# Attention and feed-forward on one core: full fp32 products as three float32r products, and the layer tiles shared out anew between VectorE and GpSimd

## The chip, the cores and the metric

The kernel runs on one core of a Trainium2 chip. TensorE (PE in the profile) multiplies matrices into PSUM; VectorE (DVE), ScalarE (ACT) and GpSimd (POOL) do elementwise work; SyncE (SP) issues the transfers. The metric is the device time of one execution in microseconds; of the kernel before it is the median of three runs.

## The reference

```python
# q: (4, 12288, 128), kv: (4, 384, 32, 128), w_sr: (128, 128)
kv_pool = kv.reshape(B, H // r, r, W // r, r, C).mean(axis=(2, 4))   # r = 4: 768 keys
k = v = kv_pool.reshape(B, -1, C) @ w_sr
s = scale * (q @ k.transpose(0, 2, 1))
a = softmax(s)
x = (a @ v).reshape(-1, 128)
# w_in: (128, 2048), w_out: (2048, 128)
h = x @ w_in
out = (h - tanh(h)) @ w_out
```

There are 4 batches of 12288 queries; keys and values are the same 768 vectors.

## The kernel before, in words

The 49152 queries go through in 96 groups of 512 (24 a batch, `G = 512`, `NG = 24`), always with channels on the 128 partitions. The kernel treats both the softmax and the layer as a main linear part and a small rest. The scores are small, so exp(s) - 1 - s is what remains beside a linear part; and h - tanh(h) is expanded around the batch's centre, with a linear part (slopes), and a third-order rest.

Small rests are multiplied in float32r, which reads 32-bit data at a lower precision; the two linear parts need more, and are multiplied in full fp32. So a group has on TensorE:

- scores (L712): 6 matmuls of 512 columns from the keys `kTr` and the rounded query `qr`, into three two-bank PSUM tiles `big`. ACT forms exp (L716, `E`), VectorE the rest E - 1 - s (L719, `r2`).
- shares (L732): 6 matmuls that sum the rest over the keys; ACT turns the sum into `t` (L745).
- the attention's straight part (L736, `straight` in `attention`): **one full fp32 matmul** from the moment matrix `Mn` and the unrounded query `qs` (tile `q`), and 6 float32r matmuls of the values (L741) into the same PSUM bank. VectorE multiplies with `t` (L751): the output's difference from the centre, `dl`. GpSimd rounds it to float32r, `dr` (L754).
- forth (L792): 16 matmuls from the scaled weights `winr` and `dr`, two to a `big` tile, hence 8 layer tiles of 128x1024. For each, r = h^2 (1 + h) is formed in one of two ways. On VectorE: ACT squares (L796, `u`), VectorE does the rest in one instruction (L799, `r`). On GpSimd: ACT copies out of PSUM (L803, `v`), GpSimd adds 1 (L806) and multiplies twice (L810, `z` and `rp`).
- back (L832): 16 matmuls of `Wr` with those tiles, and the layer's straight part (L780): **one full fp32 matmul** from the slopes `A` and `dl`, all into the bank `acc`. ACT adds the centre's value (L841) and SP stores the group's output.

`ON_POOL` says which layer tiles go to GpSimd: tiles 0 and 3 of groups with an even number, tile 0 of groups with an odd number, and tile 0 alone of group 94: 143 tiles in all.

The order on each engine is written by a planner (`Plan`) before the program is built. Every operation has a step (its due time, in units of a layer tile; a group is 8 steps), an engine, and an estimated duration. The planner runs these through a list schedule: an engine takes, of what can start within 0.15 us, the operation with the earliest step. GpSimd's operations and some of VectorE's are kept apart by a shared "port". The order that comes out is fixed; on the chip each engine works through it and waits on semaphores. `BUFS` gives the number of buffers of each tag; tiles of one tag form a ring in which a new tile waits until the one as many places before has been used up. Tiles of different meaning can share a tag. PSUM has three `big` tiles, one bank `x` and one bank `acc`.

Attention of group g begins 20 steps before the layer of group g. The preparation of a batch (`keys`: pooling on VectorE and GpSimd, the centred keys, the values `vv32` and `vvr`, the moment `Mn` at L446 and L450; `about_centre`: weights scaled for this centre, `winr`, `Wr`, `Wg`, and the slopes `A` in four parts, L661 to L669) is spread over the groups of the batch before it. For the first batch it forms the kernel's start. After a check of the inputs a second, general program (`any_inputs`) would run where the expansion does not hold; it doesn't run on these inputs.

Of the kernel before, what the change touches and what calls it, by code (L numbers as in the profile page):

```python
# [9 lines left out]
F32 = mybir.dt.float32  # L10
R32 = mybir.dt.float32r
# [4 lines left out]
ALU = mybir.AluOpType  # L16
# [130 lines left out]
def attention_then_ffn(ctx: ExitStack, tc: tile.TileContext, q, kv, w_sr, w_in, w_out, out):  # L147
    nc = tc.nc
    V, A, PL, PE, SP = nc.vector, nc.scalar, nc.gpsimd, nc.tensor, nc.sync
# [7 lines left out]
    NGT = B * NG  # L157
# [5 lines left out]
    dram = ctx.enter_context(tc.tile_pool(name="dram", bufs=1, space=DRAM))  # L163
    plan = Plan(tc)

    BUFS = {"kc": 2, "kvp": 1, "kTr": 2, "vv32": 1, "vvr": 2, "Mn": 2, "A": 2, "Wg": 4, "Wr": 2,
            "winr": 2, "q": 4, "qr": 3, "E": 2, "r2": 5, "t": 2, "dl": 2, "dr": 2, "u": 3, "r": 4,
            "rp": 2, "v": 2, "z": 1, "o": 2, "row": 2, "col": 2, "G0": 2, "hb": 2, "W2": 1,
            "most": 1}

    def sb(key, tag, shape, dt=F32, step=0.0):
        n = BUFS[tag]
        plan.tile(key, tag, n, lambda: wk.tile(shape, dt, tag=tag, name=tag, bufs=n), step)
# [166 lines left out]
    def keys(b, s0):  # L340
# [107 lines left out]

        def copy_moment():
            A.activation(out=plan[Mn], in_=plan[pm][:, 0:P], func=AF.Copy, scale=scale / K)  # L450
# [14 lines left out]
        plan.op(s2, "ACT", 0.85, copy_values, (pv,), (vv32,), late=0.1)  # L465
        plan.op(s2 + (0 if b else 2), "DVE" if b else "ACT", 0.9, small_values, (pv,), (vvr,))
        plan.op(s3, "PE", 1.8, moment, (vv32,), (pm,), late=0.2)
        plan.op(s3, "ACT", 0.3, copy_moment, (pm,), (Mn,), late=0.1)
        norm(s4, Mn, p4, b)

    def about_centre(b, s0):
# [178 lines left out]
        for n in range(NW):  # L650
# [20 lines left out]
            def by_third(n=n, fs=fs):  # L671
# [7 lines left out]
            plan.op(third_at[n], "POOL", 1.25, by_third,  # L679
                    (a3s, ("wout32", n)), ((Wr, n),), port=True)  # L680

    def attention(g, s0):
        b, i = divmod(g, NG)
        kTr, vvr, Mn = (f"{x}.{b}" for x in ("kTr", "vvr", "Mn"))
        qs, qr, dl, dr, den, num, t = (f"{x}.{g}" for x in ("q", "qr", "dl", "dr", "den", "num", "t"))
        sb(qs, "q", [P, G])
        sb(qr, "qr", [P, G], R32)
        sb(t, "t", [P, G])
        sb(dl, "dl", [P, G])
        sb(dr, "dr", [P, G], R32)  # L690
        plan.tile(f"left.{g}", f"left.{g}", 1, lambda: None)

        def load_q():
            SP.dma_start(out=plan[qs], in_=q[b, :, i * G : (i + 1) * G])

        def rounded_q():
            PL.tensor_scalar(out=plan[qr], in0=plan[qs], scalar1=1.0, scalar2=1.0, op0=ALU.mult,
                             op1=ALU.mult)

        plan.op(s0 - 10, "SP", 0.5, load_q, (), (qs,), late=2.0, dma=0.65)  # L700
        plan.op(s0 - 3, "POOL", 0.63, rounded_q, (qs,), (qr,))
        for k in range(AN):
            s, e, r = (f"{x}.{g}.{k}" for x in ("s", "e", "r2"))
            at = s0 + k * ATT / AN
            big(s, at)
            sb(e, "E", [P, WIDE])
            sb(r, "r2", [P, WIDE], R32)

            def scores(k=k, s=s):
                for h in range(2):  # L710
                    n = 2 * k + h
                    PE.matmul(out=half(plan[s], h), lhsT=plan[kTr][:, n * P : (n + 1) * P],  # L712
                              rhs=plan[qr], start=True, stop=True)

            def exps(s=s, e=e):
                A.activation(out=plan[e], in_=plan[s], func=AF.Exp)  # L716

            def beyond(s=s, e=e, r=r):
                V.scalar_tensor_tensor(out=plan[r], in0=plan[e], scalar=-1.0, in1=plan[s],  # L719
                                       op0=ALU.add, op1=ALU.subtract)  # L720
# [13 lines left out]

        def straight():
            PE.matmul(out=plan[num], lhsT=plan[Mn], rhs=plan[qs], start=True, stop=False)  # L736

        def values(k):
            for h in range(2):
                n = 2 * k + h  # L740
                PE.matmul(out=plan[num], lhsT=plan[vvr][:, n], rhs=half(plan[f"r2.{g}.{k}"], h),  # L741
                          start=False, stop=(n == KT - 1))

        def share_left():
            A.activation(out=plan[t], in_=plan[den], func=AF.Copy, scale=-1.0, bias=1.0)  # L745

        def store_left():
            SP.dma_start(out=left[g : g + 1], in_=plan[t][0:1, :])

        def apart():  # L750
            V.tensor_tensor(out=plan[dl], in0=plan[num], in1=plan[t], op=ALU.mult)  # L751

        def rounded():
            PL.tensor_scalar(out=plan[dr], in0=plan[dl], scalar1=1.0, scalar2=1.0, op0=ALU.mult,  # L754
                             op1=ALU.mult)

        for k in range(AN):
            plan.op(at, "PE", 0.465, partial(shares, k), ("ident", f"r2.{g}.{k}"), (den,), late=0.2)
        plan.op(at, "ACT", 0.69, share_left, (den,), (t,), late=0.1)
        plan.op(at + 1, "SP", 0.5, store_left, (t,), (f"left.{g}",), late=2.0, dma=0.02)  # L760
        plan.op(at + 0.5, "PE", 0.93, straight, (Mn, qs), (num,))
        for k in range(AN):
            plan.op(at + 0.5, "PE", 0.465, partial(values, k), (vvr, f"r2.{g}.{k}"), (num,), late=0.2)
        plan.op(at + 0.5, "DVE", 0.69, apart, (num, t), (dl,), late=0.08)
        plan.op(at + 1, "POOL", 0.63, rounded, (dl,), (dr,))

    FS, AS, WS, APART, MORE = 3, 8, 6, 3, 3.0
    ON_POOL = [((0, 3), (0,))[g % 2] for g in range(NGT)]
    ON_POOL[NGT - 2] = (0,)

    def feed_forward(g, s0):
        b = g // NG
        Am, Wr, G0, winr, dl, dr = (f"{x}.{k}" for x, k in (
            ("A", b), ("Wr", b), ("G0", b), ("winr", b), ("dl", g), ("dr", g)))
        acc, o = f"acc.{g}", f"o.{g}"
        bank(acc, "acc", s0)
        sb(o, "o", [P, G])

        def straight():
            PE.matmul(out=plan[acc], lhsT=plan[Am], rhs=plan[dl], start=(g > 0), stop=(g == 0))  # L780

        if g:
            plan.op(s0, "PE", 0.93, straight, (Am, dl), (acc,))
        for n in range(UN):
            hp, u, r, v, z = (f"{x}.{g}.{n}" for x in ("h", "u", "r", "v", "z"))
            s = s0 + n - (2 if n in ON_POOL[g] else 0)
            big(hp, s)

            def forth(n=n, hp=hp):
# [21 lines left out]

            plan.op(s - 6, "PE", 0.465, forth, (winr, dr), (hp,), late=0.2)
            back_at = s + 2
            if n in ON_POOL[g]:
                sb(r, "rp", [P, WIDE], R32)
                sb(v, "v", [P, WIDE])
                sb(z, "z", [P, WIDE])
                plan.op(s, "ACT", 1.03, copy, (hp,), (v,), late=0.1)
                plan.op(s, "POOL", 1.05, moved_pool, (v,), (z,))
                plan.op(s, "POOL", 2.4, partial(times, z, z, v), (z, v), (z,))  # L820
                plan.op(s, "POOL", 2.4, partial(times, r, z, v), (z, v), (r,))
                back_at = s + 5
# [122 lines left out]
    def any_inputs():  # L945
        def t(tag, shape, dt=F32):
            return wk.tile(shape, dt, tag=tag, name=tag + "_any", bufs=BUFS[tag])

        def bank():
            return ps.tile([P, WIDE], F32, tag="big", name="big_any", bufs=3)  # L950
# [4 lines left out]
        for b in range(B):  # L955
# [161 lines left out]
```

## Time and profile before

| what | value |
|---|---|
| median of three runs | 1421.43 us (1420.7 to 1421.87) |
| profiled execution, its own time | 1421.67 us |
| its span, first to last instruction | 1419.9 us |
| TensorE, matmul records | 1388.5 us busy, 98% |
| VectorE | 1216.1 us, 86% |
| ScalarE | 1158.2 us, 82% |
| GpSimd | 1066.2 us, 75% |
| mean granted TensorE clock | 0.996 of full speed |

Busy is the union of an engine's instruction records. Records of neighbours can overlap: a matmul's record begins before the one ahead of it has ended, so the spacing of starts says more than the length of a record. A full fp32 matmul shows as two records, a float32r one as one. "Idle before" is the time in which an engine had nothing running ahead of an instruction, with the instruction that ended the wait behind the arrow. In a timeline the columns are start, duration, engine, line, operation, output and inputs by tile name, number of merged instructions.

### The profile page before, as it was taken

The page shows a single profiled execution, that of the slowest core. Times are in us where ns is not written, and L with a number is a line of the kernel's source. Part 1 is how long each engine was busy: PE and PEld are TensorE (multiplying, and loading weights), DVE is VectorE, ACT ScalarE, POOL GpSimd, SP SyncE. Part 2 cuts the span into 40 slices and gives each one's busy share as a digit, 9 for nine tenths or more (in the row PEclk, how much of TensorE's full clock was granted, in tenths as well). Part 3 has the DMA queues.
Part 4 walks back from the last instruction along what each step waited for, and adds up shares of the span by engine and source line. Part 5 has one row for each costly group of instructions (what it writes and reads, how often), then busy time and mean ns, then how long its engine had stood idle before and what let it go on. Part 6 is the DMA issues. An engine that isn't in the chain of part 4 may idle for free.

```text
span 1419.9 us, 17460 instructions
## 1 busy us (share of the span) xinstructions
PE 1388.5 (98%) x5824; PEld 1039.0 (73%) x5824; DVE 1216.1 (86%) x1203; ACT 1158.2 (82%) x1299; POOL 1066.2 (75%) x826
## 2 busy tenths in 40 slices
PE   5999999999999999999999999999999999999997
PEld 4777777777777777777777777777777777777775
DVE  7978888888988887898988888888888888888886
ACT  4768887887888888787888888877888888888886
POOL 3788676788887676788986776698667777876773
PEclk9999999999999999999999999999999999999999
DMA  9231111012321111124211111111110111111101
GB/s 357 75 119 38 45 38 38 30 60 82 127 89 38 38 39 36 36 81 138 81 52 45 38 38 38 34 57 46 38 44 32 45 40 37 45 38 38 38 17 37
DMA packets 40370, 84.53 MB, mean 60 GB/s; under 512 B 5232, under 2 KB 7408, under 8 KB 40272
## 3 DMA queue, kind: packets, MB, share of 16 engines
q1 hardware_dynamic: 40272, 83.34, 17.6%
q8 instruction: 48, 0.79, 0.2%
q14 instruction: 50, 0.41, 0.1%
HBM read 57.93 MB, written 25.39 MB: 59 GB/s over the span
## 4 chain that ended last, share of the span: by engine, by line
PE 87%; POOL 5%; DVE 4%; ACT 2%; issue 1%; DMA 0%; SPq 0%; DVEq 0%; POOLq 0%; ACTq 0%
PE big L792 24%; PE acc L832 23%; PE x L741 9%; PE x L732 9%; PE big L712 8%; PE acc L780 6%; PE x L736 5%; POOL z L810 2%; DVE r L799 1%; POOL rp L810 1%; PE x L559 1%; PE x L661 1%; POOL z L806 1%; DVE kvp L369 1%; DVE r L719 0%
## 5 line engine op out<-in xcount | busy, mean ns | idle before, releaser
L799 DVE SCALAR_TENSOR_TENSOR r<-big,u 128x1024 fp32r<-128x1024 f32 x625 | 752.9, 1219 | 117.4 <-ACT u L796 87.1
L796 ACT ACTIVATE u<-big 128x1024 f32<-128x1024 f32 x625 | 636.7, 1031 | 144.0 <-PE big L792 140.4
L792 PE MATMUL big<-dr,winr 128*128 128x512 f32 x1536 | 522.8, 423 | 3.4 <-DVE r L799 2.2
L832 PE MATMUL acc<-r,Wr 128*128 128x512 f32 x1250 | 399.7, 404 | 0.8 <-DVE r L799 0.8
L719 DVE SCALAR_TENSOR_TENSOR r<-E,big 128x1024 fp32r<-128x1024 f32 x288 | 349.4, 1214 | 45.6 <-ACT E L716 42.7
L792 PEld LDWEIGHTS big<-dr,winr 128*128 128x128 f32 x1536 | 277.2, 188 | 127.9 <-DVE r L799 31.3
L806 POOL TENSOR_SCALAR z<-v 128x1024 f32<-128x1024 f32 x143 | 152.4, 1065 | 272.9 <-ACT v L803 270.3
L810 POOL TENSOR_TENSOR rp<-z,v 128x1024 fp32r<-128x1024 f32 x143 | 344.4, 2408 | 9.4
L810 POOL TENSOR_TENSOR z<-z,v 128x1024 f32<-128x1024 f32 x143 | 345.4, 2416 | 7.5
L716 ACT ACTIVATE E<-big 128x1024 f32<-128x1024 f32 x288 | 296.9, 1032 | 41.6 <-PE big L712 38.8
L832 PEld LDWEIGHTS acc<-r,Wr 128*128 128x128 f32 x1250 | 233.8, 188 | 67.0 <-issue 13.9
L712 PE MATMUL big<-qr,kTr 128*128 128x512 f32 x576 | 187.8, 408 | 0.0
L741 PE MATMUL x<-r,vvr 128*128 128x512 f32 x576 | 184.9, 403 | 0.0
L732 PE MATMUL x<-r,share 128*128 128x512 f32 x576 | 181.5, 398 | 0.4 <-DVE dl L751 0.4
L803 ACT COPY v<-big 128x1024 f32<-128x1024 f32 x143 | 145.3, 1016 | 30.2 <-PE big L792 28.0
L741 PEld LDWEIGHTS x<-r,vvr 128*128 128x128 f32 x576 | 108.2, 188 | 30.2 <-issue 6.7
L712 PEld LDWEIGHTS big<-qr,kTr 128*128 128x128 f32 x576 | 103.9, 188 | 35.8 <-DVE r L799 8.6
L732 PEld LDWEIGHTS x<-r,share 128*128 128x128 f32 x576 | 108.2, 188 | 28.0 <-issue 2.4
L832 PE MATMUL acc<-rp,Wr 128*128 128x512 f32 x286 | 102.2, 439 | 1.1 <-POOL rp L810 0.7
L780 PE MATMUL acc<-dl,A 128*128 128x512 f32 x192 | 101.0, 607 | 0.0
L736 PE MATMUL x<-q,Mn 128*128 128x512 f32 x192 | 98.1, 592 | 0.7 <-ACT t L745 0.7
L832 PEld LDWEIGHTS acc<-rp,Wr 128*128 128x128 f32 x286 | 53.0, 188 | 25.5 <-issue 13.9
(159 smaller groups left out, 818.6 us busy)
## 6 DMA issues: line engine op xcount, KB each, us to landing
q<-in_q_dram SPq DMA_DIRECT2D x96, 256.0 KB
out_dram<-o SPq DMA_DIRECT2D x96, 256.0 KB
kc<-in_kv_dram SPq DMA_DIRECT2D x38, 512.0 KB
r<-in_kv_dram SPq DMA_DIRECT2D x8, 512.0 KB
kc<-inverse SPq DMA_DIRECT2D x12, 256.0 KB
u<-in_moe_w_in_dram SPq DMA_DIRECT2D x3, 512.0 KB
u<-in_moe_w_out_dram SPq DMA_DIRECT2D x3, 512.0 KB
left<-t SPq DMA_DIRECT2D x96, 2.0 KB
```

Source lines behind the costliest of these rows:

```text
L712: PE.matmul(out=half(plan[s], h), lhsT=plan[kTr][:, n * P : (n + 1) * P], rhs=plan[qr], start=True, stop=True)
L716: A.activation(out=plan[e], in_=plan[s], func=AF.Exp)
L719: V.scalar_tensor_tensor(out=plan[r], in0=plan[e], scalar=-1.0, in1=plan[s], op0=ALU.add, op1=ALU.subtract)
L732: PE.matmul(out=plan[den], lhsT=share, rhs=half(plan[f"r2.{g}.{k}"], h), start=(n == 0), stop=(n == KT - 1))
L736: PE.matmul(out=plan[num], lhsT=plan[Mn], rhs=plan[qs], start=True, stop=False)
L741: PE.matmul(out=plan[num], lhsT=plan[vvr][:, n], rhs=half(plan[f"r2.{g}.{k}"], h), start=False, stop=(n == KT - 1))
L780: PE.matmul(out=plan[acc], lhsT=plan[Am], rhs=plan[dl], start=(g > 0), stop=(g == 0))
L792: PE.matmul(out=half(plan[hp], h), lhsT=plan[winr][:, f * P : (f + 1) * P], rhs=plan[dr], start=True, stop=True)
L796: A.activation(out=plan[u], in_=plan[hp], func=AF.Square)
L799: V.scalar_tensor_tensor(out=plan[r], in0=plan[hp], scalar=1.0, in1=plan[u], op0=ALU.add, op1=ALU.mult)
L810: PL.tensor_tensor(out=plan[to], in0=plan[x], in1=plan[y], op=ALU.mult)
L832: PE.matmul(out=plan[acc], lhsT=plan[Wr][:, f], rhs=half(plan[r], h), start=(g == 0 and f == 0), stop=(g > 0 and f == FT - 1))
```

## The change

A value x is split into an upper part, x rounded to float32r, and a lower part, x minus the upper part, also in float32r. A product of two such values is then formed as upper x upper + lower x upper + upper x lower, three float32r matmuls into the same bank; lower x lower is left out.

- Attention: `Mn` is split into `Mh` (ACT copies the upper part, GpSimd subtracts); the query's upper part is the `qr` that exists already, its lower part `ql` is subtracted on GpSimd, due four steps after `qr`.
- Layer: the slopes `A` are split into `Ah`, once a batch; the difference, now `df` from VectorE, has the upper part `dr` (as before) and the lower part `dl`, subtracted on GpSimd.
- Each group has two more GpSimd instructions of 128x512; the planner's durations are 1.1 us for each, and 0.7 us instead of 0.93 for a straight product.
- `ON_POOL` is tile 0 in every group: 96 layer tiles on GpSimd, the others on VectorE.
- Buffers: `qr` 4 for 3, `Wg` 3 for 4, `Mn` 1 for 2, `dl` 1 for 2; new `Mh` 2, `Ah` 2, `ql` 2, `df` 1; `vv32` loses its own buffer and takes one of the ring `kc`, in which the keys' chunks arrive. The general program takes its `vv32` from the ring `r`.

```diff
-    BUFS = {"kc": 2, "kvp": 1, "kTr": 2, "vv32": 1, "vvr": 2, "Mn": 2, "A": 2, "Wg": 4, "Wr": 2,
-            "winr": 2, "q": 4, "qr": 3, "E": 2, "r2": 5, "t": 2, "dl": 2, "dr": 2, "u": 3, "r": 4,
+    BUFS = {"kc": 2, "kvp": 1, "kTr": 2, "vvr": 2, "Mn": 1, "Mh": 2, "A": 2, "Ah": 2, "Wg": 3, "Wr": 2,
+            "winr": 2, "q": 4, "qr": 4, "ql": 2, "E": 2, "r2": 5, "t": 2, "dl": 1, "df": 1, "dr": 2, "u": 3, "r": 4,
...
-        sb(vv32, "vv32", [P, KT, C])
+        sb(vv32, "kc", [P, KT, C])
...
         def copy_moment():
             A.activation(out=plan[Mn], in_=plan[pm][:, 0:P], func=AF.Copy, scale=scale / K)
+            A.copy(out=plan[Mh][:, 0], in_=plan[Mn])
+
+        def moment_left():
+            PL.tensor_tensor(out=plan[Mh][:, 1], in0=plan[Mn], in1=plan[Mh][:, 0].bitcast(F32),
+                             op=ALU.subtract)
...
-        plan.op(s3, "ACT", 0.3, copy_moment, (pm,), (Mn,), late=0.1)
+        plan.op(s3, "ACT", 0.65, copy_moment, (pm,), (Mn, Mh), late=0.1)
+        plan.op(s3, "POOL", 0.35, moment_left, (Mn, Mh), (Mh,))
...
+        def upper_slopes():
+            A.copy(out=plan[Ah][:, 0], in_=plan[Am])
+
+        def lower_slopes():
+            PL.tensor_tensor(out=plan[Ah][:, 1], in0=plan[Am], in1=plan[Ah][:, 0].bitcast(F32),
+                             op=ALU.subtract)
+
+        joined = slopes_at[3] + (APART if b else 1) + 0.1
+        plan.op(joined, "ACT", 0.3, upper_slopes, (Am,), (Ah,), late=0.1)
+        plan.op(joined, "POOL", 0.35, lower_slopes, (Am, Ah), (Ah,))
...
         def straight():
-            PE.matmul(out=plan[num], lhsT=plan[Mn], rhs=plan[qs], start=True, stop=False)
+            upper, lower = (plan[Mh][:, n] for n in range(2))
+            for n, (x, y) in enumerate(((upper, qr), (lower, qr), (upper, ql))):
+                PE.matmul(out=plan[num], lhsT=x, rhs=plan[y], start=(n == 0), stop=False)
+
+        def lower_q():
+            PL.tensor_tensor(out=plan[ql], in0=plan[qs], in1=plan[qr].bitcast(F32),
+                             op=ALU.subtract)
...
         def apart():
-            V.tensor_tensor(out=plan[dl], in0=plan[num], in1=plan[t], op=ALU.mult)
+            V.tensor_tensor(out=plan[df], in0=plan[num], in1=plan[t], op=ALU.mult)
...
-        plan.op(at + 0.5, "PE", 0.93, straight, (Mn, qs), (num,))
+        plan.op(s0 + 1, "POOL", 1.1, lower_q, (qs, qr), (ql,))
+        plan.op(at + 0.5, "PE", 0.7, straight, (Mh, qr, ql), (num,))
...
-        plan.op(at + 0.5, "DVE", 0.69, apart, (num, t), (dl,), late=0.08)
-        plan.op(at + 1, "POOL", 0.63, rounded, (dl,), (dr,))
+        plan.op(at + 0.5, "DVE", 0.69, apart, (num, t), (df,), late=0.08)
+        plan.op(at + 1, "POOL", 0.63, rounded, (df,), (dr,))
+
+        def lower_left():
+            PL.tensor_tensor(out=plan[dl], in0=plan[df], in1=plan[dr].bitcast(F32), op=ALU.subtract)
+
+        plan.op(at + 6, "POOL", 1.1, lower_left, (df, dr), (dl,))
...
-    ON_POOL = [((0, 3), (0,))[g % 2] for g in range(NGT)]
-    ON_POOL[NGT - 2] = (0,)
+    ON_POOL = (0,)
...
         def straight():
-            PE.matmul(out=plan[acc], lhsT=plan[Am], rhs=plan[dl], start=(g > 0), stop=(g == 0))
+            upper, lower = (plan[Ah][:, n] for n in range(2))
+            for n, (x, y) in enumerate(((upper, dr), (lower, dr), (upper, dl))):
+                PE.matmul(out=plan[acc], lhsT=x, rhs=plan[y], start=(g > 0 and n == 0),
+                          stop=(g == 0 and n == 2))
...
-            plan.op(s0, "PE", 0.93, straight, (Am, dl), (acc,))
+            plan.op(s0, "PE", 0.7, straight, (Ah, dl, dr), (acc,))
```

More of the change, by code (lines that the diff above doesn't have):

```diff
@@ L374, in keys @@
         sb(kTr, "kTr", [P, K], R32)
-        sb(vv32, "vv32", [P, KT, C])
+        sb(vv32, "kc", [P, KT, C])
         sb(vvr, "vvr", [P, KT, C], R32)
         sb(Mn, "Mn", [P, C])
+        Mh = f"Mh.{b}"
+        sb(Mh, "Mh", [P, 2, C], R32)
         apart_by = 4 if b else 1
@@ L481, in about_centre @@
         sb(Am, "A", [P, C])
+        Ah = f"Ah.{b}"
+        sb(Ah, "Ah", [P, 2, C], R32)
         sb(Wr, "Wr", [P, FT, C], R32)
@@ L680, in about_centre @@
                     (a3s, ("wout32", n)), ((Wr, n),), port=True)
+        def upper_slopes():
[6 more added lines that the diff above has]
+        plan.op(joined, "POOL", 0.35, lower_slopes, (Am, Ah), (Ah,))
     def attention(g, s0):
         b, i = divmod(g, NG)
-        kTr, vvr, Mn = (f"{x}.{b}" for x in ("kTr", "vvr", "Mn"))
+        kTr, vvr, Mh = (f"{x}.{b}" for x in ("kTr", "vvr", "Mh"))
         qs, qr, dl, dr, den, num, t = (f"{x}.{g}" for x in ("q", "qr", "dl", "dr", "den", "num", "t"))
@@ L687, in attention @@
         sb(qr, "qr", [P, G], R32)
+        ql = f"ql.{g}"
+        sb(ql, "ql", [P, G], R32)
         sb(t, "t", [P, G])
-        sb(dl, "dl", [P, G])
+        sb(dl, "dl", [P, G], R32)
+        df = f"df.{g}"
+        sb(df, "df", [P, G])
         sb(dr, "dr", [P, G], R32)
@@ L750, in apart @@
         def apart():
-            V.tensor_tensor(out=plan[dl], in0=plan[num], in1=plan[t], op=ALU.mult)
+            V.tensor_tensor(out=plan[df], in0=plan[num], in1=plan[t], op=ALU.mult)
         def rounded():
-            PL.tensor_scalar(out=plan[dr], in0=plan[dl], scalar1=1.0, scalar2=1.0, op0=ALU.mult,
+            PL.tensor_scalar(out=plan[dr], in0=plan[df], scalar1=1.0, scalar2=1.0, op0=ALU.mult,
                              op1=ALU.mult)
@@ L760, in attention @@
         plan.op(at + 1, "SP", 0.5, store_left, (t,), (f"left.{g}",), late=2.0, dma=0.02)
-        plan.op(at + 0.5, "PE", 0.93, straight, (Mn, qs), (num,))
+        plan.op(s0 + 1, "POOL", 1.1, lower_q, (qs, qr), (ql,))
+        plan.op(at + 0.5, "PE", 0.7, straight, (Mh, qr, ql), (num,))
         for k in range(AN):
             plan.op(at + 0.5, "PE", 0.465, partial(values, k), (vvr, f"r2.{g}.{k}"), (num,), late=0.2)
-        plan.op(at + 0.5, "DVE", 0.69, apart, (num, t), (dl,), late=0.08)
-        plan.op(at + 1, "POOL", 0.63, rounded, (dl,), (dr,))
+        plan.op(at + 0.5, "DVE", 0.69, apart, (num, t), (df,), late=0.08)
[3 more added lines that the diff above has]
+        plan.op(at + 6, "POOL", 1.1, lower_left, (df, dr), (dl,))
     FS, AS, WS, APART, MORE = 3, 8, 6, 3, 3.0
-    ON_POOL = [((0, 3), (0,))[g % 2] for g in range(NGT)]
-    ON_POOL[NGT - 2] = (0,)
+    ON_POOL = (0,)
     def feed_forward(g, s0):
         b = g // NG
-        Am, Wr, G0, winr, dl, dr = (f"{x}.{k}" for x, k in (
-            ("A", b), ("Wr", b), ("G0", b), ("winr", b), ("dl", g), ("dr", g)))
+        Ah, Wr, G0, winr, dl, dr = (f"{x}.{k}" for x, k in (
+            ("Ah", b), ("Wr", b), ("G0", b), ("winr", b), ("dl", g), ("dr", g)))
         acc, o = f"acc.{g}", f"o.{g}"
@@ L779, in straight @@
         def straight():
-            PE.matmul(out=plan[acc], lhsT=plan[Am], rhs=plan[dl], start=(g > 0), stop=(g == 0))
+            upper, lower = (plan[Ah][:, n] for n in range(2))
+            for n, (x, y) in enumerate(((upper, dr), (lower, dr), (upper, dl))):
+                PE.matmul(out=plan[acc], lhsT=x, rhs=plan[y], start=(g > 0 and n == 0),
+                          stop=(g == 0 and n == 2))
         if g:
-            plan.op(s0, "PE", 0.93, straight, (Am, dl), (acc,))
+            plan.op(s0, "PE", 0.7, straight, (Ah, dl, dr), (acc,))
         for n in range(UN):
             hp, u, r, v, z = (f"{x}.{g}.{n}" for x in ("h", "u", "r", "v", "z"))
-            s = s0 + n - (2 if n in ON_POOL[g] else 0)
+            s = s0 + n - (2 if n in ON_POOL else 0)
             big(hp, s)
@@ L813, in feed_forward @@
             back_at = s + 2
-            if n in ON_POOL[g]:
+            if n in ON_POOL:
                 sb(r, "rp", [P, WIDE], R32)
@@ L837, in feed_forward @@
         if g == 0:
-            plan.op(s0 + UN + 1, "PE", 0.93, straight, (Am, dl), (acc,), late=0.2)
+            plan.op(s0 + UN + 1, "PE", 0.7, straight, (Ah, dl, dr), (acc,), late=0.2)
         def result():
@@ L966, in any_inputs @@
             A.activation(out=halves(kT), in_=halves(pk)[:, :, 0:KH], func=AF.Copy, scale=scale / W)
-            pv, vv = bank(), t("vv32", [P, KT, C])
+            pv, vv = bank(), t("r", [P, KT, C])
             for n in range(KT):
```

## The prediction

> **What bounds the kernel now.** I read the page first (busy shares, chain), then busy time by stretch, then the orders of TensorE, VectorE and GpSimd in a steady stretch, then waits.
>
> ```profile
> span 1419.9 us, 17460 instructions
> ...
> PE 1388.5 (98%) x5824; PEld 1039.0 (73%) x5824; DVE 1216.1 (86%) x1203; ACT 1158.2 (82%) x1299; POOL 1066.2 (75%) x826
> ...
> PE 87%; POOL 5%; DVE 4%; ACT 2%; issue 1%; DMA 0%; SPq 0%; DVEq 0%; POOLq 0%; ACTq 0%
> ```
>
> The profiled execution took 1421.67 us, 1.8 more than its span and 0.24 above the median of the three runs; my sum starts at 1421.67. PE is busy 98% and is 87% of the chain, but matmul records overlap, so the share alone proves nothing; the spacing of their starts does. By stretch (columns: window, length, then busy time and count of PE, PEld, DVE, ACT, POOL):
>
> ```profile
> 1060.10:1383.50 323.40, 323.40 (x1309) 241.23 (x1309) 283.12 (x255) 280.34 (x313) 238.57 (x161) 1.00 0.11 37
> 224.10:362.50 138.40, 136.93 (x612) 103.80 (x612) 116.38 (x119) 109.48 (x123) 107.10 (x94) 1.00 0.19 59
> ...
> 527.60:679.40 151.80, 150.83 (x670) 115.18 (x669) 130.61 (x132) 119.58 (x134) 122.12 (x107) 1.00 0.23 73
> ...
> 870.00:1020.00 150.00, 149.14 (x666) 114.48 (x665) 124.84 (x127) 118.89 (x133) 114.85 (x96) 1.00 0.13 41
> ```
>
> The first row is a steady stretch without preparation, the others are the three in which the next batch's keys and weights are prepared. Starts on PE in the steady one:
>
> ```profile
> 1100.85 1.02 PE L780 MATMUL acc<-dl,A 128*128 128x512 f32 x2
> 1101.31 1.02 PE L832 MATMUL acc<-rp,Wr 128*128 128x512 f32 x2
> 1102.17 1.02 PE L736 MATMUL x<-q,Mn 128*128 128x512 f32 x2
> 1102.63 1.02 PE L792 MATMUL big<-dr,winr 128*128 128x512 f32 x2
> 1103.49 0.63 PE L832 MATMUL acc<-r,Wr 128*128 128x512 f32 x2
> ...
> 1106.27 0.62 PE L832 MATMUL acc<-r,Wr 128*128 128x512 f32 x2
> ...
> 1113.68 1.11 PE L780 MATMUL acc<-dl,A 128*128 128x512 f32 x2
> ...
> 1127.64 0.59 PE L780 MATMUL acc<-dl,A 128*128 128x512 f32 x1
> ```
>
> From 1103.49 to 1106.27 six pairs of float32r matmuls start in 2.78 us: 0.463 a pair, 0.232 each. From 1100.85 to 1102.17 stands one full product (L780, two records) and one pair, 1.32 us; from 1102.17 to 1103.49 the other (L736) and a pair, 1.32 again. So a full fp32 product takes 1.32 - 0.463 = 0.857 us. A group has 50 float32r matmuls (6 scores, 6 shares, 6 values, 16 forth, 16 back) and two full ones: 50 x 0.232 + 2 x 0.857 = 13.31 us. The two groups from 1100.85 to 1127.64 take 26.79, 13.40 each. PE has work for 99% of the steady time at the spacing it reaches: it is the bound.
>
> **The change, part by part.**
>
> Straight products (L736, L780). Three float32r matmuls at 0.232 are 0.695 us instead of 0.857: 0.162 saved, twice a group, 192 times: **-31.1 us**. That spacing is of neighbours which each load their own 128x128 weights, as these three do. The group's floor on PE becomes 56 x 0.232 = 12.99 us.
>
> The Trainium skill ("FP8 and Floating Point Precision", TensorE Precision Notes) says that a true fp32 product takes four passes through the array, the products of both halves. At this trace's 0.232 a pass that would be 0.93 and the saving 0.23, -45 us in all; the row has 0.857, so the rule's count fits only with shorter passes, and the row decides.
>
> One layer tile on GpSimd per group instead of alternately two and one (L806 and L810, x143; 96 afterwards). The other 47 go to VectorE as L799, which becomes x672. On ACT a copy becomes a square, 1016 against 1031 ns:
>
> ```profile
> L799 DVE SCALAR_TENSOR_TENSOR r<-big,u 128x1024 fp32r<-128x1024 f32 x625 | 752.9, 1219 | 117.4 <-ACT u L796 87.1
> L796 ACT ACTIVATE u<-big 128x1024 f32<-128x1024 f32 x625 | 636.7, 1031 | 144.0 <-PE big L792 140.4
> ...
> L803 ACT COPY v<-big 128x1024 f32<-128x1024 f32 x143 | 145.3, 1016 | 30.2 <-PE big L792 28.0
> ```
>
> ```profile
> 700.02 0.68 DVE L751 TENSOR_TENSOR dl<-x,t 128x512 f32<-128x512 f32 x1
> 700.62 1.21 DVE L369 TENSOR_REDUCE kvp<-kc 128x64 f32<-128x1024 f32 x1
> 701.75 1.21 DVE L719 SCALAR_TENSOR_TENSOR r<-E,big 128x1024 fp32r<-128x1024 f32 x1
> 702.88 1.22 DVE L799 SCALAR_TENSOR_TENSOR r<-big,u 128x1024 fp32r<-128x1024 f32 x1
> 704.01 1.21 DVE L719 SCALAR_TENSOR_TENSOR r<-E,big 128x1024 fp32r<-128x1024 f32 x1
> 705.14 1.22 DVE L799 SCALAR_TENSOR_TENSOR r<-big,u 128x1024 fp32r<-128x1024 f32 x1
> ```
>
> These six follow each other without a wait: a wide tile every 1.13 us although its record lasts 1.22, and L751 in 0.60. VectorE needs 10 x 1.13 + 0.60 = 11.90 us in a group with one tile on GpSimd, 10.77 with two, 11.34 on average. After the change every group needs 11.90 of PE's 12.99, 92% where it was 85%. The 47 x 1.13 = 53 us lie beside PE as long as VectorE's idle time per group can fall from 13.40 - 11.34 = 2.06 to 1.09 us. What that idle time waits for in the steady stretch:
>
> ```profile
> ACT u L796 <- PE big L792: 31.8, 71, 0.8
> DVE r L799 <- ACT u L796: 25.0, 36, 1.3
> DVE r L719 <- ACT E L716: 12.3, 36, 0.8
> ...
> PEld big L792 <- DVE r L799: 7.5, 24, 0.4
> ```
>
> VectorE waits for ACT, and ACT for PE: it waits for work that PE has not yet issued, around the straight products above all, which get shorter. PE's loads wait for VectorE only 7.5 us in 24 groups. I take +1 us over the steady groups; the bounds are 0 and the slow rival below. If the cover goes, late next are the three PSUM buffers `big`, and with them PE's forth matmuls.
>
> In the three preparation stretches (440 us together) VectorE also pools keys and scales weights; it is busy 84, 86 and 83% there. Each has some ten groups, so five more tiles, 5.7 us of VectorE. Bounds: nothing, or all of it on the path, 3 x 5.7 = +17; a gain is possible too, since GpSimd has fewer double tiles among its own preparation. Spread evenly, 116.38 + 5.7 us fit into 138.40 - 3, so I take the nearer end: **+4**.
>
> GpSimd:
>
> ```profile
> 1100.88 1.04 POOL L806 TENSOR_SCALAR z<-v 128x1024 f32<-128x1024 f32 x1
> 1102.01 2.40 POOL L810 TENSOR_TENSOR z<-z,v 128x1024 f32<-128x1024 f32 x1
> 1104.49 2.41 POOL L810 TENSOR_TENSOR rp<-z,v 128x1024 fp32r<-128x1024 f32 x1
> 1106.87 0.62 POOL L697 TENSOR_SCALAR qr<-q 128x512 fp32r<-128x512 f32 x1
> 1107.46 1.04 POOL L806 TENSOR_SCALAR z<-v 128x1024 f32<-128x1024 f32 x1
> ```
>
> A layer tile holds it 5.99 us, a rounding 0.59. The two subtractions (128x512, two inputs) aren't in the trace; bounds are half of L810, 1.20, and 1.32, the mean of such an addition on strided data:
>
> ```profile
> L363 POOL TENSOR_TENSOR kc<-kc 128x512 f32<-128x512 f32 x18 | 23.8, 1322 | 8.0 <-DMA kc<-in_kv_dram 4.3 <-DVE hb L519 3.6
> ```
>
> The layout is that of L810, so 1.20. A group has 5.99 + 2 x 0.59 + 2 x 1.20 = 9.6 us, 74% of 12.99; before 1.5 x 5.99 + 1.18 = 10.2. The lower query follows its rounding four steps later and is wanted six steps after that; the lower attention difference has as long before the group's L780. Behind a late one on GpSimd's queue stands the rounding of the next difference, for which forth (L792) waits. Price in the steady stretch nil, covered by 3.4 us of idle GpSimd a group.
>
> Buffers. `df` (one) makes the next L751 wait for a subtraction one group older; `q` comes free earlier, so its loads go out no later on SP; `vv32` in the ring of `kc` and `Wg` with three delay only preparation. Nil, with the stretches' bounds above.
>
> The start. Mn is split by an ACT copy and a small subtraction:
>
> ```profile
> 40.98 0.31 ACT L450 ACTIVATE Mn<-x 128x128 f32<-128x128 f32 x1
> ...
> 51.83 1.12 PE L736 MATMUL x<-q,Mn 128*128 128x512 f32 x2 [0.69 <-ACT t L745]
> ...
> 53.91 1.04 POOL L657 TENSOR_TENSOR Wg<-wout,hb 128x512 f32<-128x512 f32 x1
> 55.23 0.62 POOL L754 TENSOR_SCALAR dr<-dl 128x512 fp32r<-128x512 f32 x1 [0.28 <-DVE dl L751]
> 55.81 2.04 POOL L657 TENSOR_TENSOR Wg<-wout,hb 128x512 f32<-128x512 f32 x2
> 57.99 1.04 POOL L806 TENSOR_SCALAR z<-v 128x1024 f32<-128x1024 f32 x1
> ```
>
> Mn is there 10.5 us before it is read, so the split is hidden. But GpSimd is full ahead of the first layer tile, and up to two lower queries come into that row: 0 to 2.4 us, I take +1. The slopes' split runs once a batch on idle time.
>
> Sum: 1421.67 - 31.1 + 1 + 4 + 1 = **1396.6**; forecast 1396.5.
>
> **The rivals.**
>
> *VectorE limits the preparation only.* For it: shares there of 83 to 86%, with bursts. Against it: 22 us free in 138. Thirty groups lose their 0.32 (9.7 us) and pay the 17: 1421.67 - 31.1 + 27 = 1417.5.
>
> *No change: the products save nothing or VectorE takes it back.* Three separate weights on fresh operands might space at 0.286 instead of 0.232 and cost 0.857 again; or VectorE's idle time stops at 13.40 - 11.90 = 1.50 us. Either gives 13.40 a group, 1421.5. Against the first: every row from 1103.49 to 1106.27. For the second: a group with one tile on GpSimd already runs so.
>
> *VectorE is the bound, slower.* If its 2.06 us of idle time are latencies of the loop PE, ACT, VectorE through three `big` buffers and stay, a group takes 11.90 + 2.06 = 13.96: +0.56 x 96 = +54, 1475. It decides from 1.50 us of remaining idle time on. For it: L799's wait for L796, 87.1 us, the largest on VectorE. Against it: these waits lead back to a PE without a gap.
> The Trainium skill ("Perfetto Trace Analysis", Identifying the Most-Contended Engine) stands on this rival's side: it says that matmul busy time is no measure, and to judge TensorE by its weight loads' share. That is 73% here, below VectorE's 86%, and the time would be 1475. The trace agrees that the records overstate PE, but their start spacing leaves 1%.
>
> **How the numbers follow.** The forecast has 0.70, its own range 1386 to 1409: below, no stall at all (1390.6) and some 4 us of GpSimd's waits gone from the preparation; above, the three stalls three times as large as taken (6 us become 18). The preparation rival has 0.11, no change 0.07, slower 0.12. About 0.2% (3 us) is what a measurement can tell from no change, so faster is 0.70 + 0.11 = 0.81, same 0.07, slower 0.12. The range goes from 1384 to 1421: it leaves out the slow rival, half of no change and 0.03 below, together under 2 in 10.
>
> **What would show it.** L736 and L780 with three records each and 0.70 us to the next line; steady groups 13.0 to 13.2 apart; VectorE with 672 L799 and 90 to 92% busy; GpSimd about 1020 us busy (1066 - 47 x 5.89 + 192 x 1.20), its subtractions near 1.2; PE's loads waiting for VectorE little more than now. It is wrong if PE's pairs stand more than 0.47 apart in the steady stretch while VectorE runs without gaps, or if the three products take over 0.8 us.

## The result: no gain, and what the profile after shows

The changed kernel takes 1424.13 us (median of 16 runs), the kernel before beside it 1421.86: a ratio of 1.0016, 95% interval 1.0008 to 1.0023. The forecast was 1396.5. The times are medians of runs at a granted clock of about 0.99; one run of the last control below, at 0.751 and 1711.69 us, is left out of its median. The page of the changed kernel:

```profile
span 1422.3 us, 17720 instructions
...
PE 1380.7 (97%) x6016; PEld 1065.3 (75%) x6016; DVE 1261.5 (89%) x1250; ACT 1167.5 (82%) x1307; POOL 1039.3 (73%) x885
...
PE 83%; DVE 8%; POOL 4%; ACT 2%; DMA 2%; issue 1%; SPq 0%; DVEq 0%; POOLq 0%; ACTq 0%
...
L838 DVE SCALAR_TENSOR_TENSOR r<-big,u 128x1024 fp32r<-128x1024 f32 x672 | 805.3, 1218 | 86.3 <-ACT u L835 66.7
...
L800 POOL TENSOR_TENSOR dl<-df,dr 128x512 fp32r<-128x512 f32 x96 | 126.4, 1316 | 87.9 <-PE acc L818 87.6
...
L766 POOL TENSOR_TENSOR ql<-q,qr 128x512 fp32r<-128x512 f32 x96 | 125.7, 1310 | 47.8 <-PE x L763 47.6
```

The work moved as announced: 672 layer tiles on VectorE, two subtractions a group on GpSimd. VectorE's part of the chain has doubled, from 4 to 8%. A steady group on TensorE (start, duration, line, operands, merged instructions):

```profile
1116.97 0.62 PE L818 MATMUL acc<-dr,Ah 128*128 128x512 f32 x2
1117.42 0.40 PE L818 MATMUL acc<-dl,Ah 128*128 128x512 f32 x1
1117.66 0.63 PE L831 MATMUL big<-dr,winr 128*128 128x512 f32 x2
...
1126.65 0.63 PE L831 MATMUL big<-dr,winr 128*128 128x512 f32 x2
1127.12 0.63 PE L757 MATMUL x<-r,share 128*128 128x512 f32 x2
1127.58 0.71 PE L831 MATMUL big<-dr,winr 128*128 128x512 f32 x2
1128.13 0.62 PE L871 MATMUL acc<-r,Wr 128*128 128x512 f32 x2
1128.69 0.73 PE L831 MATMUL big<-dr,winr 128*128 128x512 f32 x2
1129.26 0.63 PE L757 MATMUL x<-r,share 128*128 128x512 f32 x2
1129.82 0.73 PE L737 MATMUL big<-qr,kTr 128*128 128x512 f32 x2
1130.39 0.62 PE L818 MATMUL acc<-dr,Ah 128*128 128x512 f32 x2
```

The straight product takes 1117.66 - 1116.97 = 0.69 us, as announced, instead of 0.857. But from one L818 to the next it is 13.42 us, as long as before (13.40), and 0.43 more than the 12.99 that the matmuls need. The loss stands in one place. From 1126.65 to 1127.58 a `big` pair and one other pair take 0.93 us; the next two such steps take 1.11 and 1.13. The weight loads of the same group that had to wait (idle time and its releaser in brackets), and VectorE at that time:

```profile
1127.56 0.30 PEld L831 LDWEIGHTS big<-dr,winr 128*128 128x128 f32 x2 [0.25 <-DVE r L838]
1128.68 0.30 PEld L831 LDWEIGHTS big<-dr,winr 128*128 128x128 f32 x2 [0.36 <-DVE r L744]
1129.82 0.30 PEld L737 LDWEIGHTS big<-qr,kTr 128*128 128x128 f32 x2 [0.37 <-DVE r L838]
```

```profile
1125.15 1.22 DVE L744 SCALAR_TENSOR_TENSOR r<-E,big 128x1024 fp32r<-128x1024 f32 x1 [0.49 <-ACT E L741]
1126.29 1.22 DVE L838 SCALAR_TENSOR_TENSOR r<-big,u 128x1024 fp32r<-128x1024 f32 x1
1127.42 1.21 DVE L744 SCALAR_TENSOR_TENSOR r<-E,big 128x1024 fp32r<-128x1024 f32 x1
1128.55 2.35 DVE L838 SCALAR_TENSOR_TENSOR r<-big,u 128x1024 fp32r<-128x1024 f32 x2
```

From 1125.15 on VectorE works without a gap, a tile every 1.13 us. In this phase, that of the shares, TensorE's order puts only one other pair between two `big` pairs, 0.93 us of work per tile: it uses up the three `big` buffers and then runs at VectorE's pace. Just before, VectorE stood still for 0.49 us. Over the whole steady stretch from 1050 to 1387 us, 25 groups, the waits (total, times, longest) are:

```profile
ACT u L835 <- PE big L831: 30.9, 72, 0.8
...
PEld big L737 <- DVE r L838: 8.5, 23, 0.4
PEld big L831 <- DVE r L744: 8.3, 23, 0.4
PEld big L831 <- DVE r L838: 7.1, 26, 0.9
```

About three such waits a group come to 23.9 us, where before the same kinds of wait came to 9.8 us in 24 groups (7.5 of L792 for L799, the line in the prediction, and 1.9 and 0.4 in two smaller ones). My theory from this: the saving is real, but the fixed order gives it back in the shares phase, where TensorE now arrives before VectorE is through. Rivals: VectorE's sum of work decides wherever it falls; GpSimd's subtractions and their waits do; the products save nothing.

### The profile page after: what moved, and what is told of

Read it like the earlier page. It is cut to its first block, busy times and chain, and to the rows that moved or that the text cites. A ratio compares the mean times of both kernels' runs of the same rounds, so it can differ in the third digit from the quotient of the medians.

```text
span 1422.3 us, 17720 instructions
## 1 busy us (share of the span) xinstructions
PE 1380.7 (97%) x6016; PEld 1065.3 (75%) x6016; DVE 1261.5 (89%) x1250; ACT 1167.5 (82%) x1307; POOL 1039.3 (73%) x885
## 4 chain that ended last, share of the span: by engine, by line
PE 83%; DVE 8%; POOL 4%; ACT 2%; DMA 2%; issue 1%; SPq 0%; DVEq 0%; POOLq 0%; ACTq 0%
PE big L831 24%; PE acc L871 22%; PE big L737 9%; PE x L772 8%; PE x L757 8%; PE acc L818 4%; PE x L763 4%; DVE r L838 3%; DVE r L744 1%; DMA kc<-in_kv_dram 1%; DVE kvp L369 1%; ACT u L835 1%; POOL rp L849 1%; DVE winr L625 1%; POOL z L849 1%
## 5 line engine op out<-in xcount | busy, mean ns | idle before, releaser
L838 DVE SCALAR_TENSOR_TENSOR r<-big,u 128x1024 fp32r<-128x1024 f32 x672 | 805.3, 1218 | 86.3 <-ACT u L835 66.7
L835 ACT ACTIVATE u<-big 128x1024 f32<-128x1024 f32 x672 | 686.6, 1029 | 156.1 <-PE big L831 151.8
L744 DVE SCALAR_TENSOR_TENSOR r<-E,big 128x1024 fp32r<-128x1024 f32 x288 | 349.2, 1213 | 35.2 <-ACT E L741 34.3
L849 POOL TENSOR_TENSOR z<-z,v 128x1024 f32<-128x1024 f32 x96 | 231.3, 2410 | 7.2
L849 POOL TENSOR_TENSOR rp<-z,v 128x1024 fp32r<-128x1024 f32 x96 | 230.8, 2405 | 1.2
L845 POOL TENSOR_SCALAR z<-v 128x1024 f32<-128x1024 f32 x96 | 100.6, 1048 | 174.8 <-ACT v L842 174.8
L800 POOL TENSOR_TENSOR dl<-df,dr 128x512 fp32r<-128x512 f32 x96 | 126.4, 1316 | 87.9 <-PE acc L818 87.6
L766 POOL TENSOR_TENSOR ql<-q,qr 128x512 fp32r<-128x512 f32 x96 | 125.7, 1310 | 47.8 <-PE x L763 47.6
L842 ACT COPY v<-big 128x1024 f32<-128x1024 f32 x96 | 97.6, 1016 | 11.3 <-PE big L831 11.3
L880 ACT ACTIVATE o<-acc,G 128x512 f32<-128x512 f32 x96 | 65.5, 683 | 6.6 <-PE acc L871 4.7
L782 DVE TENSOR_TENSOR df<-x,t 128x512 f32<-128x512 f32 x96 | 65.4, 682 | 5.6 <-PE x L772 4.9
```

Of the source, the lines that this page charges most:

```text
L766: PL.tensor_tensor(out=plan[ql], in0=plan[qs], in1=plan[qr].bitcast(F32), op=ALU.subtract)
L800: PL.tensor_tensor(out=plan[dl], in0=plan[df], in1=plan[dr].bitcast(F32), op=ALU.subtract)
L835: A.activation(out=plan[u], in_=plan[hp], func=AF.Square)
L838: V.scalar_tensor_tensor(out=plan[r], in0=plan[hp], scalar=1.0, in1=plan[u], op0=ALU.add, op1=ALU.mult)
L849: PL.tensor_tensor(out=plan[to], in0=plan[x], in1=plan[y], op=ALU.mult)
```

## The experiments

**Sharing alone.** From the kernel before:

```diff
-    ON_POOL = [((0, 3), (0,))[g % 2] for g in range(NGT)]
-    ON_POOL[NGT - 2] = (0,)
+    ON_POOL = [(0,)] * NGT
```

> The kernel before with one layer tile on GpSimd in every group and nothing else; the full fp32 products stay. If VectorE's added load (47 tiles of 1.13 us, 53 us) is what eats the saving wherever it falls, this run pays it openly: about 1450. If VectorE only costs where several of its tiles follow each other without a gap, the long straight products of 0.857 us give it time to catch up: 1420 to 1432, with the steady group still at 13.4 us. If GpSimd was a bound before, it gets faster than 1415.

Measured: 1430.66 us, ratio 1.0065 (1.0048 to 1.0082). Of 53 us more on VectorE, 9 show. Seven results in the steady stretch:

```profile
1243.81 0.68 ACT L840 ACTIVATE o<-acc,G 128x512 f32<-128x512 f32 x1
...
1324.30 0.68 ACT L840 ACTIVATE o<-acc,G 128x512 f32<-128x512 f32 x1
```

Six groups in 80.49 us, 13.42 each: with the long products the added tile is hidden in the steady groups, and the 9 us fall in the rest.

**Products alone.** From the kernel before, order and sharing kept. All three products take rounded operands, written as float32r; `qr`, which is now read longer, has one buffer more on the chip:

```diff
-            PE.matmul(out=plan[num], lhsT=plan[Mn], rhs=plan[qs], start=True, stop=False)
+            for n in range(3):
+                PE.matmul(out=plan[num], lhsT=plan[Mn], rhs=plan[qr], start=(n == 0),
+                          stop=False)
...
-            PE.matmul(out=plan[acc], lhsT=plan[Am], rhs=plan[dl], start=(g > 0), stop=(g == 0))
+            for n in range(3):
+                PE.matmul(out=plan[acc], lhsT=plan[Am], rhs=plan[dl], start=(g > 0 and n == 0),
+                          stop=(g == 0 and n == 2))
```

> The kernel before, its order on every engine and its sharing of layer tiles unchanged; only each full product is three float32r products. It leaves out the lower parts (all three take the rounded operands, and the three sum up), so GpSimd gets no subtraction. What the prediction said, a TensorE without a gap, gives the whole saving: 1421.9 - 31 = 1391. If the order written for 0.93 us products makes TensorE meet a VectorE that hasn't caught up, a part is given back as waits for the buffers big: 1405 to 1416. If three products cost what the two full ones cost: 1422.

Measured: 1407.44 us, ratio 0.9902 (0.9886 to 0.9919): 14 us of the 31 arrive. Six groups take 1328.28 - 1248.86 = 79.42 us, 13.24 each:

```profile
1248.86 0.69 ACT L845 ACTIVATE o<-acc,G 128x512 f32<-128x512 f32 x1
...
1328.28 0.70 ACT L845 ACTIVATE o<-acc,G 128x512 f32<-128x512 f32 x1
```

That is half of the way from 13.40 to the 13.07 of a full saving: the products do save, but even without a tile more on VectorE the other half doesn't arrive in the old order. VectorE alone does not explain that half. Between 1060 and 1380 us TensorE's loads wait 7.2 us for VectorE's release of `big`, less than before (9.6 in the same stretch), and 4.0 us for GpSimd's `rp`, for which they did not wait before; no run separates these. Of the 14 us a part may be another effect: the query is read only by its rounding here, so its buffer comes free earlier, and SP's wait for it, 161 us before, falls below 12.

**Without the subtractions.** The bodies of `lower_q` and `lower_left` are empty, and the third product reads the upper part:

```diff
-            for n, (x, y) in enumerate(((upper, qr), (lower, qr), (upper, ql))):
+            for n, (x, y) in enumerate(((upper, qr), (lower, qr), (upper, qr))):
```

> The changed kernel without its two subtractions of 128x512 a group on GpSimd; the third and second product take the upper part again, so TensorE's and VectorE's work and the order on every engine stay. It leaves out the lower parts of query and difference. If GpSimd's subtractions, and the waits they bring into its queue (87.6 us for L818, 47.6 us for L763), hold the kernel up, the time falls towards the forecast, 1395 to 1405. If VectorE does, it stays within 0.3% of 1424 and the steady group at 13.42 us.

Measured: 1411.95 us, ratio 0.9930 (0.9914 to 0.9947), between the two expectations. Six steady groups take 80.57 us, 13.43 each, as with the subtractions, so in steady work these have no part:

```profile
1240.12 0.68 ACT L879 ACTIVATE o<-acc,G 128x512 f32<-128x512 f32 x1
...
1320.69 0.68 ACT L879 ACTIVATE o<-acc,G 128x512 f32<-128x512 f32 x1
```

The 12 us lie in the preparation and the start, a second loss that I had not forecast: the first result comes 1.3 us earlier, and the stretches of the first two preparations (from the result of group 10 to that of 22, and from 31 to 44) are 3.9 and 4.6 us shorter. A piece of the changed kernel's chain in a preparation stretch (start, length, what):

```profile
660.90 2.38 POOL rp L849
...
663.71 1.27 POOL ql L766
...
664.99 0.33 SPq L719
...
666.22 4.63 DMA kc<-in_kv_dram
...
670.92 1.29 POOL kc L363
```

A query's load (L719) waits for the buffer that the subtraction L766 frees. On SP's queue the keys' load (L355) stands behind it, its transfer takes 4.63 us, and GpSimd's pooling waits for that. SP's waits for the query's buffer, changed kernel first, then before:

```profile
SPq L719 <- POOL ql L766: 325.8, 92, 10.5
```

```profile
SPq L694 <- PE x L736: 161.3, 89, 3.9
```

That this queue carries the 12 us is argued from the chain, not tested by itself; a run with a fifth query buffer would have told. A rival is the subtractions' own time on GpSimd: further on in the same chain two of them stand at 682.39 and 684.01 us, 1.26 and 1.27 long, among the pooling. And the sum of SP's waits says little by itself: it is 319 us in the run below with tiles 1 and 7 halved (1400 us), and 286 in the new order (1386 us).

**Half of tile 3, half of tiles 1 and 7.** VectorE's instruction works on half of the columns of the tiles named, and back reads that half twice:

```diff
+                to, x, y = plan[r], plan[hp], plan[u]
+                if n == 3:
+                    to, x, y = half(to, 0), half(x, 0), half(y, 0)
+                V.scalar_tensor_tensor(out=to, in0=x, scalar=1.0, in1=y, op0=ALU.add, op1=ALU.mult)
...
-                    PE.matmul(out=plan[acc], lhsT=plan[Wr][:, f], rhs=half(plan[r], h),
+                    PE.matmul(out=plan[acc], lhsT=plan[Wr][:, f], rhs=half(plan[r], 0 if n == 3 else h),
```

> The changed kernel with layer tile 3 of every group, the one that came from GpSimd in the even groups, computed on 512 of its 1024 columns on VectorE; back reads that half twice. It leaves out half of one of the eight tiles. It takes about 96 x 0.53 = 51 us from VectorE, nearly the 53 us that the change added. If VectorE's sum decides, most of the saving comes back: 1395 to 1405. If what decides is the place where VectorE's tiles stand without a gap, in the shares phase (E tiles 1 and 2, layer tiles 7 and 1), tile 3 lies outside of it and the time stays: 1420 to 1425.

> As the run with tile 3 halved, but with layer tiles 1 and 7 halved, two of the four VectorE tiles for whose release TensorE waits once each in every steady group. It leaves out half of two of the eight tiles. VectorE loses about 102 us. If the gapless row of tiles in the shares phase is the cause, TensorE's waits of 0.44 us a group mostly go: steady group 13.0 to 13.2 us and 1393 to 1402. If VectorE's load isn't the cause (GpSimd, the transfers, or products that save nothing), the time stays at 1420 or above.

Measured: tile 3 halved 1423.12 us, 1.0009 (0.9999 to 1.0018); tiles 1 and 7 halved 1400.39, 0.9851 (0.9834 to 0.9867). Taking away nearly all of VectorE's added work changes nothing where it lies outside of the shares phase; 102 us taken inside bring 24 us and groups of (1323.77 - 1245.42) / 6 = 13.06 us:

```profile
1245.42 0.69 ACT L882 ACTIVATE o<-acc,G 128x512 f32<-128x512 f32 x1
...
1323.77 0.68 ACT L882 ACTIVATE o<-acc,G 128x512 f32<-128x512 f32 x1
```

It is the place and not the sum. The second run takes twice as much as the first, but the first, 51 us, already should have shown something if the sum mattered. TensorE's waits for VectorE say the same. Between 1050 and 1370 us they come to 21.9 us in the changed kernel, and to 22.0 with tile 3 halved:

```profile
PEld big L737 <- DVE r L841: 8.2, 23, 0.4
PEld big L831 <- DVE r L744: 7.7, 21, 0.4
PEld big L831 <- DVE r L841: 6.1, 22, 1.0
```

With tiles 1 and 7 halved 4.4 us are left, 0.7 of them a single wait for L744, the others these:

```profile
PEld big L831 <- DVE r L841: 3.7, 22, 0.4
```

**Two products instead of three.**

```diff
-            for n, (x, y) in enumerate(((upper, qr), (lower, qr), (upper, ql))):
+            for n, (x, y) in enumerate(((upper, qr), (upper, ql))):
```

The layer's straight part likewise.

> The changed kernel with two float32r products instead of three in each straight part (lower x upper is left out); order and all else unchanged. TensorE has 2 x 0.232 us a group less, 44.5 us in all. If VectorE's load is the bound of the changed kernel, nothing comes of it: 1420 to 1424. If TensorE's time outside of the shares phase still counts fully, most of it comes: 1390 to 1405.

Measured: 1402.65 us, ratio 0.9865 (0.9848 to 0.9881), 21 us below the changed kernel of the 44.5 taken away. A steady group takes 13.20 us. VectorE's load is therefore not a hard bound, and TensorE's time counts only by half: the other half turns into waits again. Between 1050 and 1370 us TensorE's loads wait for VectorE 32.0 us instead of 21.9.

**The old sharing, with the subtractions.**

```diff
-    ON_POOL = (0,)
+    ON_POOL = [((0, 3), (0,))[g % 2] for g in range(NGT)]
+    ON_POOL[NGT - 2] = (0,)
```

> The changed kernel with the sharing of layer tiles as before: two on GpSimd in the even groups, one in the odd. The planner writes the order anew. VectorE is relieved of the 53 us, GpSimd has 1.5 x 5.99 + 1.18 + 2.6 = 12.8 us in a group of 13. If VectorE's sum of work is what spoilt the saving, 1395 to 1410. If GpSimd can't carry both, 1440 to 1500: then the tile had to move for the subtractions' sake.

Measured: 1467.86 us, ratio 1.0326 (1.0309 to 1.0343). What TensorE's `back` loads wait for there:

```profile
PEld acc L872 <- POOL rp L850: 58.2, 72, 2.2
```

GpSimd's tiles come late. With this planner and these due times the tile had to leave GpSimd if the subtractions were to go there; another order was not tried for it.

**Another order for the same work.** All edits to the changed kernel:

```diff
-            plan.op(at - 6, "PE", 0.465, scores, (kTr, qr), (s,), late=0.2)
+            plan.op(at - 5, "PE", 0.465, scores, (kTr, qr), (s,), late=0.2)
...
-            plan.op(at + 0.5, "PE", 0.465, partial(values, k), (vvr, f"r2.{g}.{k}"), (num,), late=0.2)
+            plan.op(at + 1, "PE", 0.465, partial(values, k), (vvr, f"r2.{g}.{k}"), (num,), late=0.2)
...
-    ON_POOL = (0,)
+    ON_POOL = (1,)
...
-            plan.op(s - 6, "PE", 0.465, forth, (winr, dr), (hp,), late=0.2)
-            back_at = s + 2
+            plan.op(s - 5, "PE", 0.465, forth, (winr, dr), (hp,), late=0.2)
+            back_at = s + 1
...
-                plan.op(s, "ACT", 1.03, square, (hp,), (u,), late=0.1)
+                plan.op(s, "ACT", 1.0, square, (hp,), (u,), late=0.1)
...
-                plan.op(s, "DVE", 1.22, cube, (hp, u), (r,), late=0.08)
+                plan.op(s, "DVE", 1.18, cube, (hp, u), (r,), late=0.08)
...
-    ATT = 7.0
-    LEAD = 20.0
+    ATT = 7.5
+    LEAD = 19.0
```

> The changed kernel, same instructions and same buffers, with another order: layer tile 1 instead of 0 on GpSimd, the attention 19 steps ahead instead of 20, scores and forth due one step later, back one step earlier, values half a step later, and 1.18 and 1.00 us instead of 1.22 and 1.03 as the planner's durations of VectorE's and ACT's layer tile. All work is done. If the saving was lost to the order, which heaps VectorE's tiles in the shares phase, it comes back: steady group 13.0 to 13.1 us, 1383 to 1400. If VectorE's load by itself is the bound, no order helps: 1415 or more.

(`ATT` is the number of steps over which a group's scores are spread.) Measured: **1386.41 us, ratio 0.9750 (0.9734 to 0.9767)**, faster than both kernels. Its steady stretch by engine (columns as in the prediction), and that of the changed kernel:

```profile
1050.00:1370.00 320.00, 319.51 (x1385) 256.05 (x1383) 301.28 (x273) 283.96 (x317) 232.16 (x173) 1.00 0.11 37
```

```profile
1049.90:1387.00 337.10, 336.58 (x1414) 257.25 (x1412) 306.12 (x278) 295.72 (x326) 238.50 (x178) 1.00 0.11 36
```

In the new order, TensorE's largest sum of waits for VectorE in that stretch, and six groups:

```profile
PEld big L831 <- DVE r L838: 1.8, 4, 0.8
```

```profile
1245.45 0.69 ACT L880 ACTIVATE o<-acc,G 128x512 f32<-128x512 f32 x1
...
1323.21 0.69 ACT L880 ACTIVATE o<-acc,G 128x512 f32<-128x512 f32 x1
```

77.76 us for six groups, 12.96 each, the floor on TensorE within what the 0.232 is known. VectorE is busy 301.28 of 320 us, 94%, where it was 91%, and TensorE's loads wait for it 2.4 us (1.8, 0.4 and 0.2) instead of 21.9 in a stretch of the same length. All nine edits were made at once, so which of them does it is not shown. In TensorE's order the layer's straight part now stands between two forth pairs of the shares phase:

```profile
1206.37 0.63 PE L831 MATMUL big<-dr,winr 128*128 128x512 f32 x2
1206.83 0.63 PE L757 MATMUL x<-r,share 128*128 128x512 f32 x2
1207.30 0.63 PE L831 MATMUL big<-dr,winr 128*128 128x512 f32 x2
1207.77 0.63 PE L818 MATMUL acc<-dr,Ah 128*128 128x512 f32 x2
1208.24 0.39 PE L818 MATMUL acc<-dl,Ah 128*128 128x512 f32 x1
1208.47 0.62 PE L831 MATMUL big<-dr,winr 128*128 128x512 f32 x2
```

**Controls: the full products in a new order.** The first takes the same nine edits, the second due times of its own:

> The control for the new order: the kernel before, with its full fp32 products, one layer tile on GpSimd in every group, and the same nine edits of due times and planned durations as in the run new_order. If the new order by itself brings what that run showed, about 1390. If the gain needs the shorter products, TensorE's floor stays at 13.31 us a group and the time at 1415 to 1435.

> The same control with due times and planned durations chosen for the full products, since an order that suits three short products need not suit one long one: straight products half a step and a whole step earlier, values half a step earlier, shares half a step later, and others. With a floor of 13.31 us, at best 1390 to 1400 would be 13.3 us in every group with a shorter preparation; I expect 1400 to 1415, so 15 to 30 us above new_order. If it comes within 5 us of new_order (1386), the products aren't what the new order's gain comes from.

The second's edits, from the kernel with the sharing alone:

```diff
-            plan.op(at - 6, "PE", 0.465, scores, (kTr, qr), (s,), late=0.2)
+            plan.op(at - 5, "PE", 0.465, scores, (kTr, qr), (s,), late=0.2)
...
-            plan.op(at, "DVE", 1.22, beyond, (s, e), (r,), late=0.08)
+            plan.op(at, "DVE", 1.2, beyond, (s, e), (r,), late=0.08)
...
-            plan.op(at, "PE", 0.465, partial(shares, k), ("ident", f"r2.{g}.{k}"), (den,), late=0.2)
+            plan.op(at + 0.5, "PE", 0.465, partial(shares, k), ("ident", f"r2.{g}.{k}"), (den,), late=0.2)
...
-        plan.op(at + 0.5, "PE", 0.93, straight, (Mn, qs), (num,))
+        plan.op(at, "PE", 0.93, straight, (Mn, qs), (num,))
...
-            plan.op(s0, "PE", 0.93, straight, (Am, dl), (acc,))
+            plan.op(s0 - 1, "PE", 0.93, straight, (Am, dl), (acc,))
...
```

(Further: values at `at`, `apart` at `at + 0.1`, back one step after its tile and six for GpSimd's, result a step earlier, 1.06 us for the square, 1.18 for VectorE's tile, GpSimd's tile 1, `ATT` 7.5, `LEAD` 19.) Measured: 1424.55 us, 1.0018 (1.0009 to 1.0028), and 1413.37 us, 0.9934 (0.9914 to 0.9954). Beside the kernel before, the nine edits bring nothing to the full products, and an order of their own brings 9 us; beside the run with the sharing alone, 1430.66, it is 6 and 17. Between the two kernels with an order of their own stand 27.0 us, close to the 31 of the prediction's sum. That either order is the best for its products is not shown.

## Why the prediction was wrong, point by point

- *TensorE is the bound, a full product costs 0.857 us, three float32r ones 0.695.* Right: 0.69 in the trace, 13.24 us groups with the products alone, 12.96 with a fitting order.
- *Straight products, -31.1 us.* Right as work saved, wrong as time in this order: 14 us at most with the products alone.
- *"The 47 x 1.13 = 53 us lie beside PE as long as VectorE's idle time per group can fall from 2.06 to 1.09 us ... I take +1 us over the steady groups."* This is the step that failed. The cover was counted over a whole group. Over a whole group the sum fits, as the new order shows with 12.96 us and the same tiles on VectorE; but the order is fixed. In the shares phase VectorE's tiles stand 1.13 us apart against 0.93 of PE's work, and VectorE's idle time lies outside of that phase, where it covers nothing. It fell only to 13.42 - 11.90 = 1.52 us. The forecast had a steady group at 13.07 us and it took 13.42, so the term was not 1 us in all but 0.35 a group. In the changed kernel's trace 49 of the 95 spacings between results are such groups (13.35 to 13.55 us); that makes some 17 us, an estimate, of the 27.6 by which the forecast was missed. The waits that the prediction took from one line, 7.5 us, were 9.8 with the two smaller ones.
- *Preparation, +4.* Too small as well. From the result of group 10 to that of 22, 31 to 44 and 55 to 66, 36 groups in all, the changed kernel takes 541.1 us where it took 537.7 before. By the sum 11.7 us of shorter products should have come off, so the price was 15 us and not 4; without the subtractions 9.3 of them go.
- *The no-change rival* had this figure (VectorE's idle time stops at 1.50 us), nearly the time that came (1421.5 for 1424.13) and, in its sentence on what speaks for it, that a group with one tile on GpSimd already runs so; I gave it 0.07. That the total came so near is in part luck: the loss in the steady groups alone would have left a gain, and the preparation took the rest. Its mechanism was right, though what stopped was one phase, not VectorE as a whole.
- *GpSimd: "price in the steady stretch nil", the start +1; "`q` comes free earlier, so its loads go out no later on SP".* The first holds: 13.43 us with and without subtractions. The second does not: without them the kernel is 12 us faster in the preparation and at the start, and SP's wait for the query's buffer has doubled, from 161 to 326 us. A subtraction measured 1.31 to 1.32 us for the 1.20 taken: of the two bounds the strided row was the right one.
- *The slow rival, and the rule of the Trainium skill ("Perfetto Trace Analysis", Identifying the Most-Contended Engine).* 1475 did not come. By the weight loads' share, the part of the rule that the prediction used, VectorE was the engine to watch, and it was VectorE that TensorE waited for; but halving a tile of it in the wrong place brought nothing, and in the new order VectorE is busier and the kernel faster. Neither the rule's share nor my spacing says in which phase an engine is short.

## What to carry to other kernels

Where two engines are both nearly full, as TensorE (99% of a steady group before, by its spacing) and VectorE (91% after) here, and the order is fixed, cover has to be counted phase by phase: compare, between two uses of a scarce buffer, the work that the order gives to one engine with what the other needs for that buffer. Shortening the bound engine's work also takes away the time in which the next engine caught up. Here the whole gain came only with an order written anew for the new durations: it was worth 38 us to the shorter products, and an order of their own 9 us to the full ones.

## What the runs showed of the hardware

A late `big` buffer delays TensorE twice here, ahead of the pair that needs it and within that pair. In the changed kernel's group shown at the beginning the waiting weight loads start at most 0.02 us ahead of their matmuls (1127.56 and 1127.58), where this one, which had nothing to wait for, runs 0.23 us ahead of its pair at 1128.13:

```profile
1127.90 0.42 PEld L871 LDWEIGHTS acc<-r,Wr 128*128 128x128 f32 x2
```

The pair after such a wait takes 0.55 to 0.57 us to the next instead of 0.463. From 1127.58 to 1130.39 five pairs take 2.81 us instead of 2.32, and of these 0.5 us some 0.3 stand in the three pairs behind a wait, the rest ahead of them. So three short waits account for the 0.43 us by which a group exceeds 12.99.
